# Token-major q features turned by DMA transposes for three of eight batches, and a new order from step 781 on, in a fused linear-attention and FFN kernel

## The chip, the cores and the metric

The kernel runs on one core of a Trainium2 chip. The time is that of the core, in microseconds (us) of the device. TensorE (PE) does the matmuls, VectorE (DVE) and ScalarE (ACT) the element-wise work, GpSimd (POOL) and SyncE (SP) start most of the DMA transfers here. Each engine takes its instructions in the order in which they were issued to it.

## The reference

Linear attention with an exponential feature map ("hedgehog"), 8 batches of 8 heads with 576 tokens and a head size of 64, 128 features; then an FFN with a squared relu over all 4608 tokens, 512 to 2048 to 512.

```python
def phi(x):
    proj = np.einsum('bhsd,df->bhsf', x, w_phi)
    proj = proj - np.max(np.abs(proj), axis=-1, keepdims=True)
    return np.concatenate([np.exp(proj), np.exp(-proj)], axis=-1)
q_p, k_p = (phi(q), phi(k))
kv = np.einsum('bhsf,bhsd->bhfd', k_p, v)
z = np.sum(k_p, axis=2)
num = np.einsum('bhsf,bhfd->bhsd', q_p, kv)
den = np.einsum('bhsf,bhf->bhs', q_p, z)[..., None] + 1e-06
attn = num / den                      # then x: [4608, 512], heads side by side
h = np.maximum(x @ w_in, 0.0)
return h * h @ w_out
```

For q the maximum of a token is the same in numerator and denominator but for the sign of the projection, so the kernel takes exp(+proj) and exp(-proj) without subtracting and corrects the second relative to the first by a small factor, exp(-2 max), per token and head.

## The kernel before

**Staging.** Batch b's k, q and v are loaded on POOL's queue (L253, L261, L273), in pieces, into double buffers `xk`, `xq`, `xv` (index b % 2), as tokens by head features in bf16. From batch 2 on one crossbar DMA on SP (L338) turns all of k, another all of q, into `kT` and `qT`: 18 blocks of 128x128, in which the two halves of the 128 rows hold two heads' features of 64.

**Attention of a batch** works on five blocks of tokens and heads, c = 0 to 3 (1024 columns each: 128 tokens by 8 groups) and c = 4 (half as wide, the last 64 tokens of each head).
- k: `project` (L354) makes the projection with tokens on the rows, DVE takes its maximum (L409), ACT the two exponentials `kp`, `kn` (L415), DVE scales v (L442), and PE adds up the 65-column products into kv (L472, L477).
- q: `qmax_ops` projects the q block with tokens on the rows (L354, "Pq"), DVE takes the maximum (L514, "Mq") and the PSUM banks are given back; ACT makes the correction factor `en` (L521). `q_ops` then projects the same q block a second time with features on the rows (L549, "Fq": two matmuls with up to 512 columns, on the upper and the lower 64 rows of the array), because the out heads need features on the rows; ACT takes the two exponentials from PSUM into `qp` and `qn` (L564), rings of three buffers.
- `out_ops`: eight matmuls over `qp` (L579, "NA"), DVE multiplies by `en` in PSUM (L591, "SA"), eight more over `qn` ("NB"), then the reciprocal of the denominator (L599, "rd") and the product (L603, "xo"). From batch 1 on a crossbar DMA on SP (L637) turns `xo` into `xT` (c = 0 to 3) or, for the left-over tokens, `xS` (c = 4); four blocks each.

**FFN.** Chunks of 512 tokens: chunk b takes all of batch b's `xT`, chunk 8 the 64 left-over tokens of every batch. `ffn_in` (L719, four matmuls of 512 columns per step, 16 steps) goes through relu (ACT L694 or DVE L696) and the square (DVE L703) to `h2`; `ffn_out` (L784, four matmuls per step, 16 steps) goes through a copy (L195, L197) to a store on SP (L803). Chunk 0 is taken tile by tile (L730).

**What sets the order.** The functions only record steps in a `Plan`. `ORDER` is a list of all 1731 steps written out in the code: the steps are issued in that order, and each engine keeps its part of it. `BASES` names the PSUM banks of each group, `STATES` the engine where there is a choice, and `GATES` makes a load wait for a chosen ACT or DVE step besides its buffer. Across engines only data and buffers make a step wait. So PE weaves FFN matmuls of chunk b-1 and b-2 between the attention steps of batch b and b-1. SP's queue holds, in `ORDER`'s sequence, the k and q transposes of the next batch, the `xT` and `xS` transposes of this one, and the stores.

Of the kernel before, what the change touches and what calls it, by code (L numbers as in the profile page):

```python
# [7 lines left out]
F32 = mybir.dt.float32  # L8
# [3 lines left out]
ACT = mybir.ActivationFunctionType  # L12
# [12 lines left out]
def dve_cost(n):  # L25
    return n / 960 + 0.064, n / 960 + 0.150 + SEM
# [85 lines left out]
def kernel(  # L112
# [41 lines left out]
    def sb(name, shape, dt=BF16):  # L154
        return pool.tile([P, *shape], dt, name=name)

    def ring(name, n, shape, dt=BF16):
        return [sb(f"{name}{i}", shape, dt) for i in range(n)]
# [19 lines left out]
    qp, qn = ring("qp", NQP, [8 * P]), ring("qn", NQP, [8 * P])  # L178
# [4 lines left out]
    mkn = sb("mkn", [36], F32)  # L183
# [132 lines left out]
    def attention(b):  # L316
# [181 lines left out]

        def qmax_ops(c):
# [17 lines left out]
            add("DVE", dve_cost(2 * n * Fd), fn, r=[pj], w=[("mq", s2, c)], closes=pj, what="Mq")  # L517
# [13 lines left out]

        qfeat = {}
# [128 lines left out]
        else:  # L661
# [17 lines left out]
            kv_ops(3)  # L679
            for c in range(5):  # L680
                qmax_ops(c)
            for c in range(5):
                q_ops(c)
                out_ops(c)
# [320 lines left out]
```

## Time and profile before

| | |
|---|---|
| time of the runs | 355.16 us median of 3 (354.82 to 355.61) |
| span of the profiled execution | 353.0 us, 8396 instructions |
| span of the profile against the median | 2.16 us below it; what lies around the span is not in the profile |
| L784 `ffn_out` matmuls | 128.4 us, x527 recorded |
| L719 `ffn_in` matmuls | 106.1 us, x448 recorded |
| L564 exponentials `qp`, `qn` | 37.4 us each, x40 each |
| L514 maximum of q | 44.1 us, x40 |
| L549 second projection of q | 14.9 us, x80 |
| transposes on SP: `kT`, `qT`, `xT`, `xS` | 6, 6, 28, 7 |
| medians from issue to landing of these | 5.5, 5.3, 2.7, 4.8 us |

The page gives busy times by engine over the span, and the chain of work that ended last. Rows of a line give its count, its busy time and the mean time of one. A matmul's own duration (379 ns for 512 columns) overlaps with the next one's, so what a step costs TensorE is read from the chain, where each piece has its start, its length and its count. A DMA's issue occupies the queue of the engine that starts it; its landing is counted from the start of the issue.

### The profile page before, as it was taken

Reading aid. Unit: us, or ns where it says so; the run is one execution under the profiler, and the core shown is the slowest. Engines: PE = TensorE matmul, PEld = TensorE weight load, DVE = VectorE, ACT = ScalarE, POOL = GpSimd, SP = SyncE. Lnnn points to the kernel's source line nnn. Section 1 sums busy time; section 2 is a strip of 40 time slices with the busy share of each in tenths; the row PEclk is TensorE's granted clock in tenths of the full one; section 3 lists DMA queues with packets and bytes.
Section 4 is the critical chain, followed back from the end, with each engine's and each line's share of the span. In section 5 each row is a group of like instructions: output and inputs, shape, how many; then the busy total and the mean of one; then the engine's idle time right before and its main releaser. Section 6 shows DMA issues by size and latency. Waiting matters only on the chain.

```text
span 353.0 us, 8396 instructions
## 1 busy us (share of the span) xinstructions
PE 340.7 (97%) x3367; PEld 192.2 (54%) x3400; DVE 276.1 (78%) x524; ACT 226.8 (64%) x428; POOL 96.6 (27%) x144
## 2 busy tenths in 40 slices
PE   8889999999999999999999999999999999999995
PEld 5679875544654554545445654455555544444452
DVE  4999998899979988989678888799988727736210
ACT  4999887499688875785678577869676211340301
POOL 8745350488429300297001820000000000000000
PEclk9999999999999999999999999999999999999999
DMA  9999999899989976899354995600211211010105
GB/s 102 177 200 202 196 107 155 134 142 175 182 169 150 155 141 155 160 111 158 79 129 84 120 187 111 146 20 21 53 40 53 47 51 48 30 59 2 59 3 176
DMA packets 96101, 39.59 MB, mean 112 GB/s; under 512 B 64576, under 2 KB 91584, under 8 KB 96064
## 3 DMA queue, kind: packets, MB, share of 16 engines
q0 software_dynamic: 45216, 18.36, 45.6%
q1 hardware_dynamic: 50528, 20.42, 26.5%
q8 instruction: 26, 0.43, 0.5%
q10 hardware_dynamic: 320, 0.30, 0.3%
q14 instruction: 11, 0.09, 0.1%
HBM read 36.77 MB, written 9.44 MB: 131 GB/s over the span
## 4 chain that ended last, share of the span: by engine, by line
PE 79%; DVE 8%; ACT 6%; DMA 3%; issue 2%; SPq 0%; POOL 0%; DVEq 0%; ACTq 0%; POOLq 0%
PE psum L784 30%; PE psum L719 28%; PE psum L579 5%; PE psum L354 4%; PE psum L472 3%; PE psum L730 3%; PE psum L549 2%; DVE va L442 2%; DMA xq<-in_q_dram 1%; DVE mq L514 1%; ACT kp L415 1%; ACT kn L415 1%; DMA out_dram<-ot 1%; DVE mk L388 1%; DVE h L703 1%
## 5 line engine op out<-in xcount | busy, mean ns | idle before, releaser
L784 PE MATMUL psum<-wout,h 128*128 128x512 bf16 x527 | 128.4, 379 | 3.2 <-issue 1.3
L719 PE MATMUL psum<-xT,win 128*128 128x512 bf16 x448 | 106.1, 379 | 0.1
L694 ACT ACTIVATE hr<-psum 128x512 bf16<-128x512 f32 x96 | 55.3, 596 | 46.3 <-PE psum L719 24.3
L784 PEld LDWEIGHTS <-h 128*128 128x128 bf16 x560 | 50.2, 98 | 55.2 <-issue 2.0
L719 PEld LDWEIGHTS <-win 128*128 128x128 bf16 x512 | 47.4, 97 | 53.7 <-issue 3.1
L703 DVE TENSOR_TENSOR h<-hr 128x512 bf16<-128x512 bf16 x143 | 55.9, 415 | 16.4 <-ACT hr L694 15.6
L564 ACT ACTIVATE qp<-psum 128x1024 bf16<-128x1024 f32 (+1 forms) x40 | 37.4, 940 | 21.9 <-PE psum L549 21.5
L514 DVE TENSOR_REDUCE mq<-psum 128x8 f32<-128x1024 f32 (+1 forms) x40 | 44.1, 1110 | 4.0 <-PE psum L354 3.2
L409 DVE TENSOR_REDUCE mk<-psum 128x8 f32<-128x1024 f32 (+1 forms) x35 | 38.1, 1110 | 3.1 <-PE psum L354 3.1
L415 ACT ACTIVATE kp<-psum 128x1024 bf16<-128x1024 f32 (+1 forms) x35 | 32.8, 937 | 11.6 <-DVE mk L409 8.9
L564 ACT ACTIVATE qn<-psum 128x1024 bf16<-128x1024 f32 (+1 forms) x40 | 37.4, 939 | 1.3 <-PE psum L579 1.0
L696 DVE TENSOR_SCALAR hr<-psum 128x512 bf16<-128x512 f32 x48 | 32.6, 686 | 6.5 <-PE psum L719 5.2
L253 POOL DMA_DIRECT2D xv<-in_v_dram x26 | 19.4, 763 | 51.3 <-DVE va L442 48.0
L415 ACT ACTIVATE kn<-psum 128x1024 bf16<-128x1024 f32 (+1 forms) x35 | 32.8, 936 | 0.0
L442 DVE TENSOR_TENSOR va<-xv,va 64x256 bf16<-64x256 bf16 (+2 forms) x68 | 30.4, 462 | 1.6 <-ACT va L434 0.8
L591 DVE TENSOR_TENSOR psum<-psum,en 128x520 f32<-128x520 f32 (+1 forms) x40 | 27.6, 699 | 3.9 <-PE psum L579 2.5
L603 DVE TENSOR_TENSOR xo<-psum,rden 128x512 bf16<-128x512 f32 (+1 forms) x40 | 27.3, 686 | 1.0 <-DVE rden L599 0.2
L197 ACT ACTIVATE ot<-psum 128x512 f32<-128x512 f32 x18 | 10.7, 595 | 27.1 <-PE psum L784 27.1
L195 DVE COPY ot<-psum 128x512 f32<-128x512 f32 x17 | 11.5, 684 | 15.2 <-PE psum L784 7.9
L253 POOL DMA_DIRECT2D xk<-in_k_dram x28 | 20.6, 743 | 8.4 <-ACT va L428 4.0
L472 PE MATMUL psum<-va,kp 128*128 128x65 bf16 x256 | 19.6, 193 | 0.8 <-DVE va L442 0.4
L472 PE MATMUL psum<-va,kn 128*128 128x65 bf16 x256 | 19.6, 193 | 0.0
(69 smaller groups left out, 403.4 us busy)
## 6 DMA issues: line engine op xcount, KB each, us to landing
out_dram<-ot SPq DMA_DIRECT2D x32, 256.0 KB, 2.7
xk<-in_k_dram POOLq DMA_DIRECT2D x26, 128.0 KB, 4.3
xq<-in_q_dram POOLq DMA_DIRECT2D x24, 128.0 KB, 5.5
xv<-in_v_dram POOLq DMA_DIRECT2D x24, 128.0 KB, 4.2
win<-in_moe_w_in_dram POOLq DMA_DIRECT2D x4, 512.0 KB, 11.3
wout<-in_moe_w_out_dram POOLq DMA_DIRECT2D x4, 512.0 KB, 11.7
xq<-in_q_dram POOLq DMA_DIRECT2D x4, 256.0 KB, 5.8
xv<-in_v_dram POOLq DMA_DIRECT2D x2, 512.0 KB, 9.3
```

The costliest lines, as they stand in the source:

```text
L253: pin(nc.gpsimd.dma_start(out=x[:, a * 512 : z * 512].rearrange("p (h x) -> p h x", x=4 * D), in_=src[b][2 * a : 2 * z, 0:512, :].rearrang ...
L409: pin(nc.vector.tensor_reduce(out=mk_view(g), in_=ps2(pj)[:, :, : n * Fd].rearrange("p e (i f) -> p e i f", f=Fd), axis=AX.X, op=ALU.max, ...
L415: pin(nc.scalar.activation(out=dst[slot][:, :, :n, :].rearrange("p e i f -> p e (i f)"), in_=ps2(pj)[:, :, : n * Fd], func=ACT.Exp, scale= ...
L442: pin(engine().tensor_tensor(out=t[:, :, :D].rearrange("p m (x c) -> p m x c", c=2), in0=x.rearrange("p (m x c) -> p m x c", m=n, c=2), in ...
L472: pin(nc.tensor.matmul(out=o[:, sg, hi, :], lhsT=(kp, kn)[sg][kgroup[pr]][:, j % 2, 2 * hi + j // 2, :], rhs=va[s2][sg][:, 8 * pr + 4 * hi ...
L514: pin(nc.vector.tensor_reduce(out=mqb[:, c, :, :n], in_=ps2(pj)[:, :, : n * Fd].rearrange("p e (i f) -> p e i f", f=Fd), axis=AX.X, op=ALU ...
L564: pin(nc.scalar.activation(out=o, in_=i_, func=ACT.Exp, scale=sgn))
L694: pin(nc.scalar.activation(out=hr[sl], in_=ps1(g), func=ACT.Relu))
L696: pin(nc.vector.tensor_scalar(out=hr[sl], in0=ps1(g), scalar1=0.0, scalar2=None, op0=ALU.max))
L703: pin(engine().tensor_tensor(out=dst, in0=i_, in1=i_, op=ALU.mult))
L719: pin(nc.tensor.matmul(out=o, lhsT=win[mc // 4][:, kc, mc % 4 * P : (mc % 4 + 1) * P], rhs=x, start=(kc == 0), stop=(kc == KC - 1)))
L784: pin(nc.tensor.matmul(out=ps1(g), lhsT=h2[c % 2][mc // 4][:, mc % 4, tt * P : (tt + 1) * P], rhs=wout[mc // 4][:, mc % 4, :], start=(mc = ...
```

## The change

For batches 5, 6 and 7 (`LATE = 5`):
- `qmax_ops` keeps the token-major projection in PSUM after the maximum; ACT takes the two exponentials from it, into the load buffer of the same batch that has already been turned: `xk` for even c, `xq` for odd c. Then SP turns both at once by a crossbar DMA of 16 blocks into the feature ring (for c = 4 by two of 4 blocks). `q_ops` is not called: its 15 groups of two matmuls are gone. The transpose waits for the exponentials and for the ring buffer, the next use of the load buffer (by the block c+2, and by the loads two batches later) for the transpose.
- Each block's maximum and `out_ops` are recorded one after the other instead of all maxima first; the number of steps stays the same.

For all batches `qp` and `qn` become the two halves of one ring `qf` of three buffers, and a tile `mkn` that nothing used goes. `ORDER` is a new one from its 781st step on (about 131 us in the trace before), with the `BASES` and `STATES` that belong to it. In `GATES` two entries differ: 1365 (a small load of q of batch 7) waits for 1030 instead of 1027, the same ACT step under its new number, and 1371 (a small load of v of batch 7) for 1377, the first k exponential of batch 7, instead of 1043.

```diff
+    LATE = 5
-    qp, qn = ring("qp", NQP, [8 * P]), ring("qn", NQP, [8 * P])
+    qf = ring("qf", NQP, [2, 8 * P])
+    qp, qn = [t[:, 0, :] for t in qf], [t[:, 1, :] for t in qf]
...
-    mkn = sb("mkn", [36], F32)
...
-            add("DVE", dve_cost(2 * n * Fd), fn, r=[pj], w=[("mq", s2, c)], closes=pj, what="Mq")
+            turned = b >= LATE
+            add("DVE", dve_cost(2 * n * Fd), fn, r=[pj], w=[("mq", s2, c)] + [pj] * turned, closes=None if turned else pj, what="Mq")
+            if turned:
+                slot = qslot[0] % NQP
+                qslot[0] += 1
+                qfeat[c] = slot
+                src, qx = (("xk", xk), ("xq", xq))[c % 2]
+                qe = qx[s2][:, : 16 * P].rearrange("p (u x) -> p u x", u=2)
+                held = of(src, b, (0, 1, 2, 3, "s"))
+                for u, sgn in enumerate((1.0, -1.0)):
+                    def fn(u=u, sgn=sgn):
+                        i_, o = ps2(pj)[:, :, : n * Fd], qe[:, u, : 2 * n * Fd]
...
+                        pin(nc.scalar.activation(out=o, in_=i_, func=ACT.Exp, scale=sgn))
+                    add("ACT", act_cost(2 * n * Fd), fn, r=[pj], w=[pj] + held, closes=pj if u else None, what="Eq")
+                def fn():
+                    if c == 4:
+                        for u in range(2):
+                            pin(nc.sync.dma_start_transpose(out=qf[slot][:, u, : 4 * P].rearrange("f (x p) -> f x p", p=P),
+                                                            in_=qe[:, u, : 4 * Fd]))
+                    else:
+                        pin(nc.sync.dma_start_transpose(out=qf[slot].rearrange("f u (x p) -> f (u x) p", p=P),
+                                                        in_=qx[s2][:, : 16 * P]))
+                add("SP", (2.5 if c < 4 else 2.0, 0), fn, r=held, w=[("qp", slot), ("qn", slot)],
+                    dma=(3.2 * n / 4, HW_IN, "x", "kq"), what="Xf")
...
+            if b < LATE:
+                for c in range(5):
+                    qmax_ops(c)
             for c in range(5):
-                qmax_ops(c)
-            for c in range(5):
-                q_ops(c)
+                if b < LATE:
+                    q_ops(c)
+                else:
+                    qmax_ops(c)
                 out_ops(c)
```

On SP's queue the changed order puts, from there on: batch 4's four `xT`; batch 5's features c=0, batch 6's k and q, batch 5's c=1 to 4; batch 5's `xT` (c=1, 0, 3, 2); batch 7's k; batch 6's features c=1, 0, 3, 2, between them batch 6's `xT` c=0, then c=1, batch 7's q, c=3; batch 6's features c=4 and `xT` c=2; batch 7's features c=0 to 4; batch 7's `xT` (c=2, 1, 3, 0), with the `xS` transposes and the stores between.

More of the change, by code (lines that the diff above doesn't have):

```diff
@@ L497, in q_ts @@
             return [(8 * (c // 2) + 4 * (c % 2) + i) if pe_in else 8 * (c % 2) + 2 * i + c // 2 for i in range(4)]
+        qfeat = {}
         def qmax_ops(c):
@@ L516, in fn @@
                     axis=AX.X, op=ALU.max, apply_absolute_value=True))
-            add("DVE", dve_cost(2 * n * Fd), fn, r=[pj], w=[("mq", s2, c)], closes=pj, what="Mq")
+            turned = b >= LATE
[11 more added lines that the diff above has]
+                        if c == 4:
+                            o, i_ = o.rearrange("p (i e f) -> p e i f", e=2, f=Fd), i_.rearrange("p e (i f) -> p e i f", f=Fd)
+                        else:
+                            o = o.rearrange("p (e x) -> p e x", e=2)
+                        pin(nc.scalar.activation(out=o, in_=i_, func=ACT.Exp, scale=sgn))
+                    add("ACT", act_cost(2 * n * Fd), fn, r=[pj], w=[pj] + held, closes=pj if u else None, what="Eq")
+                def fn():
+                    if c == 4:
+                        for u in range(2):
[6 more added lines that the diff above has]
+                    dma=(3.2 * n / 4, HW_IN, "x", "kq"), what="Xf")
             if c < 4:
@@ L530, in qmax_ops @@
                     add("ACT", act_cost(4), fn, r=[("mq", s2, 4)], w=[("en", s2, 4, hi)], what="en")
-        qfeat = {}
         def q_ops(c):
@@ L679, in attention @@
             kv_ops(3)
+            if b < LATE:
+                for c in range(5):
+                    qmax_ops(c)
             for c in range(5):
-                qmax_ops(c)
-            for c in range(5):
-                q_ops(c)
+                if b < LATE:
+                    q_ops(c)
+                else:
+                    qmax_ops(c)
                 out_ops(c)
@@ L948 @@
     '7762205543351613247724322302602306674447442731320126074760270660422244446264622606176160063720462403'
-    '6376440226246040224115440556605777123504024764140002202442402462567677750767766755006425602422242222'
-    '6400041712301603166777067742404660026444202224400017210165317677737366646061634664004006640006224525'
-    '2454225454357220664133466404400220620232550535444304162615557154625737570741465213753727542242756523'
-    '160'
+    '6376440226246040224115440556605777123504024764140002202442402262567677750767766755204205410045062426'
+    '0664224775446104061020510106426177640624244241032170310667601716700240233720440644667745476653763010'
+    '2631260442223066600400642345222624372543324021104562724003135227670272366751147320753641'
 )
@@ L955 @@
     '0000000000000000010100110100110100010010000010000010000000000000100000001000100010100111000000001000'
-    '0010000000001010000000100010000101010000100010010001001001111111000110010000001000110100100101000010'
-    '011000000101100101001001111100011100100101111010010100010000111111000100001'
+    '0010000000001010000000100010000101011000000001000100000011101000100001001000001110000000100111001001'
+    '010000000101001010110011000000101000010110000000100001010000110101000110000'
 )
```

166 rows, old and new, of tables (GATES, ORDER) are left out of this document.

## The prediction

> **What bounds the kernel now.** I read the busy times first, then the chain of waits that ended last, then the idle time stage by stage.
>
> ```profile
> PE 340.7 (97%) x3367; PEld 192.2 (54%) x3400; DVE 276.1 (78%) x524; ACT 226.8 (64%) x428; POOL 96.6 (27%) x144
> PEclk9999999999999999999999999999999999999999
> PE 79%; DVE 8%; ACT 6%; DMA 3%; issue 2%; SPq 0%; POOL 0%; DVEq 0%; ACTq 0%; POOLq 0%
> PE psum L784 30%; PE psum L719 28%; PE psum L579 5%; PE psum L354 4%; PE psum L472 3%; PE psum L730 3%; PE psum L549 2%; DVE va L442 2%; DMA xq<-in_q_dram 1%; DVE mq L514 1%; ACT kp L415 1%; ACT kn L415 1%; DMA out_dram<-ot 1%; DVE mk L388 1%; DVE h L703 1%
> ```
>
> TensorE is busy for 97% of the span and is 79% of the chain; the two FFN matmuls alone are 58%, and L549, the projection that the change drops for three batches, is 2%. So an instruction that leaves TensorE shortens the kernel by its whole time, unless a wait takes its place. How little waiting there is now, the windows over the part whose order changes show; their columns are the length, the busy time of PE, PEld, DVE, ACT, POOL (with counts), the granted clock, DMA share and GB/s.
>
> ```profile
> 133.00:160.00 27.00, 26.63 (x250) 13.64 (x251) 24.32 (x38) 19.47 (x36) 12.50 (x19) 1.00 0.86 141
> 160.00:190.00 30.00, 29.00 (x274) 15.14 (x275) 24.50 (x46) 21.21 (x41) 5.06 (x8) 1.00 0.76 125
> 190.00:220.00 30.00, 29.52 (x307) 15.84 (x308) 24.91 (x47) 20.55 (x36) 10.89 (x16) 1.00 0.84 120
> 220.00:250.00 30.00, 29.67 (x288) 15.75 (x289) 26.62 (x50) 23.62 (x47) 0.00 (x0) 1.00 0.28 68
> 250.00:297.00 47.00, 46.63 (x406) 24.24 (x409) 33.59 (x67) 21.89 (x39) 0.00 (x0) 1.00 0.18 47
> ```
>
> Length less PE busy is 0.37, 1.00, 0.48, 0.33 and 0.37 us: 2.55 us idle in 164 us. There is no old stall worth having; any new one adds to the time. DVE is at 90% in the first window and ACT at 65 to 79%: both have room, DVE little. From 297 on attention is over and the FFN runs alone; the change reaches that part only through its start.
>
> **What it removes.** Each L549 group is a pair of matmuls that run on the two row halves together. Its price is the step of the chain in which it stands.
>
> ```profile
> 203.78 0.22 PE psum L549 x2
> ...
> 209.04 0.86 PE psum L784 x4
> 209.91 0.25 PE psum L579 x8
> 210.15 0.33 PE psum L354 x8
> ```
>
> A pair costs 0.22 us. Batches 5 to 7 have 15 pairs, four with 512 columns and one with 256 per batch: 12 × 0.22 + 3 × 0.11 = 2.97, say **−2.9 us**. Everything else TensorE does stays. The same rows give the yardstick for what follows: a full matmul is 0.86 / 4 = 0.216 us, a group of eight out heads (L579) 0.25, of eight projections (L354) up to 0.33.
>
> **What it moves between ACT and DVE.** The 30 exponentials keep their shape and number; they now read the token-major projection that the maximum already read, so it stays in PSUM for two exponentials more, while the second pair of banks, which held the feature-major projection for the same two, is not opened at all.
>
> ```profile
> 247.98 1.02 ACT L564 ACTIVATE qp<-psum 128x1024 bf16<-128x1024 f32 x1 [1.39 <-PE psum L549]
> 248.90 1.02 ACT L564 ACTIVATE qn<-psum 128x1024 bf16<-128x1024 f32 x1
> ```
>
> Two follow each other in 0.92 us, so 1.8 us of holding moves from one bank pair to another. Cost 0. But the exponentials of block c+2 overwrite the buffer that the transpose of block c reads, so they wait for its landing, with their bank held and ACT's later relus queued behind; I allow +0.4 us (0 to 1.8, one pair of exponentials late). The merged ring of features and the unused tile that goes cost no instruction.
>
> **What it adds: 18 crossbar transposes on SP** (12 of 16 blocks; 6 of 4 blocks). The trace has 18 and 4 blocks:
>
> ```profile
> L338 SPq DMA_TRANSPOSE kT<-xk x1: 2401/2401/2401, 141.7 to 141.7; - x1
> DMA to landing us min/median/max: 4.6/4.6/4.6
> ...
> L338 SPq DMA_TRANSPOSE kT<-xk x1: 4903/4903/4903, 111.1 to 111.1; - x1
> DMA to landing us min/median/max: 11.0/11.0/11.0
> ```
>
> So 16 blocks hold SP for some 2.4 us and land after 4.6; among other traffic it can be 4.9 and 11.0. For SP that is an estimated 12 × 2.4 + 6 × 1.2 = 36 us more over three batches, on a queue that has room, but in order: a transpose that waits stops the xT transposes behind it, and with them the next FFN chunk.
>
> In sentences of its own: the Trainium skill, "DMA: Bandwidth & Descriptors", section "Latency and other measured facts", gives crossbar transposes an effective 261 GB/s, which for the 512 KB of 16 blocks would be about 2.0 us (an estimate); the clean row says 4.6 us, and the row decides. By the page's figure the ring's wait below would be 0 and the sum 0.3 us smaller.
>
> **The waits that this makes.** What an xT transpose takes depends on the loads beside it. Its rows, with POOL's burst of loads:
>
> ```profile
> L637 SPq DMA_TRANSPOSE xT<-xo x1: 1191/1191/1191, 178.3 to 178.3; - x1
> DMA to landing us min/median/max: 2.3/2.3/2.3
> ...
> L637 SPq DMA_TRANSPOSE xS<-xo x1: 1171/1171/1171, 202.7 to 202.7; - x1
> DMA to landing us min/median/max: 5.8/5.8/5.8
> ...
> L637 SPq DMA_TRANSPOSE xT<-xo x1: 1257/1257/1257, 203.9 to 203.9; - x1
> DMA to landing us min/median/max: 6.5/6.5/6.5
> ...
> L637 SPq DMA_TRANSPOSE xT<-xo x1: 2208/2208/2208, 206.8 to 206.8; - x1
> DMA to landing us min/median/max: 5.8/5.8/5.8
> ...
> L637 SPq DMA_TRANSPOSE xT<-xo x1: 1191/1191/1191, 210.0 to 210.0; - x1
> DMA to landing us min/median/max: 3.1/3.1/3.1
> ```
> ```profile
> 199.29 1.41 POOL L253 DMA_DIRECT2D xv<-in_v_dram  x2 [1.42 <-ACT hr L694]
> ...
> 203.40 0.71 POOL L253 DMA_DIRECT2D xk<-in_k_dram  x1
> 204.09 0.72 POOL L273 DMA_DIRECT2D xq<-in_q_dram  x1
> ```
>
> Alone 2.3 us; within a burst of loads 5.8 and 6.5, and 2 us after its last issue (204.1 + 0.7) still 5.8; 5 us after, 3.1. Before it, an out-head block goes through DVE:
>
> ```profile
> L603 DVE TENSOR_TENSOR xo<-psum,rden 128x512 bf16<-128x512 f32 (+1 forms) x40 | 27.3, 686 | 1.0 <-DVE rden L599 0.2
> L599 DVE RECIPROCAL rden<-psum 128x8 f32<-128x8 f32 (+1 forms) x40 | 7.9, 199 | 6.9 <-PE psum L579 6.6
> ```
>
> *Chunk 4.* In the changed order, between batch 4's last needed out heads (c=1) and chunk 4's first matmul TensorE has 16 full matmuls and three small attention groups: 16 × 0.216 + 0.6 = 4.1 us. The path beside it: reciprocal 0.20, xo 0.69, one xT issue ahead 1.2, landing 2.3 = 4.4 us. Alone it is 0.3 us late, with 5.8 us 3.8 late. The remaining loads of batch 6 stand on POOL up to there; I take the lower middle, **+1.5** (0.3 to 3.8).
>
> *Chunk 5.* After batch 5's c=2 out heads come 24 full matmuls and three projections, 24 × 0.216 + 3 × 0.33 = 6.2 us. The path: 0.20, two xo's 1.38, one issue, of which 0.5 lies beside the second xo, 0.7, landing 2.3 = 4.6: clean it is hidden. But the k and q buffers of batch 7 are the ones that batch 5 now writes its exponentials into, so batch 7's k and q loads cannot start before batch 5's last feature transposes land, and twelve loads then follow each other just as these xT transposes go. With 5.8 to 6.5 us the path is 8.1 to 8.8, and the wait 1.9 to 2.6. I take the row of the burst, **+2.0** (0 to 2.6).
>
> *Ring of three feature buffers.* The transpose for c=3 cannot start before c=0's second out heads are done. In batch 5, 4.9 us of TensorE work (20 full matmuls, a projection, a head group) stand between; the path is 4.6. I take +0.3 (0 to 6.1, the 11.0 row).
>
> *Chunk 6.* The two transposes of batch 6's c=4 stand on SP directly ahead of its last xT: 2.4 us more in front. Cover 4.8 us, path 0.9 + 2.4 + 2.3 = 5.6 if SP reaches them late, 3.2 if early. I take +0.5 (0 to 0.8).
>
> *Old waits.* Of the 1.81 us that TensorE idles from 160 to 250 some are of the old order and go; half, **−0.9** (−1.8 to 0).
>
> Sum: −2.9 + 0.4 + 1.5 + 2.0 + 0.3 + 0.5 − 0.9 = **+0.9 us**; I add 0.4 for ACT and DVE, which get the exponentials in shorter stretches (0 to 1): +1.3. The profiled execution spans 353.0 us, so 354.3; the runs' median is 355.16, 2.16 above the span for what lies around it, and I carry the difference over: **356.5 us**.
>
> **The rivals.**
>
> *The transfers hide.* Xo and loads do not meet, each crossbar lands in 2.3 or 4.6 us: the chunk waits are 0.3 and 0, and of the other terms only 0.4 + 0.3 remain. −2.9 + 0.3 + 0.7 = −1.9: 353.3; with the old waits gone too 352.3, and the TensorE saving alone gives 352.3 as well. For it: the clean landings at 141.7 and 178.3, and an idle DMA (share 0.18 to 0.28) from 220 on. Against it: nothing in the changed order but buffer reuse keeps batch 7's loads away from batch 5's xT, and it puts them together.
>
> *Pile-up at batch 7's k.* Its loads wait for batch 5's last transposes (two issues, 3.9 us in all), then 12 issues of 0.72 (8.6), a landing under load of 5.8, the k transpose 4.6: 22.9 us, while TensorE has 24 groups of four full matmuls (20.8) and 2 us of small ones before the first k projection of batch 7: 22.8. From there on every microsecond decides: with the 11.0 us row, 6.4 more, and batch 6's feature transposes queue behind it on SP. 356.5 + 5 = 361.5, as part of the wait lies beside chunk 5's.
>
> *No change.* The chunk waits just eat the saving, or batch 5 to 7 are bound by DVE (26.62 of 30 us busy from 220 to 250), which loses nothing: 355.2.
>
> *A clock that falls.* The granted clock is 9 in all slices and 1.00 in every window above, with up to 1.00 us idle in one. A wait of 3.8 us before chunk 4 would be longer than any here. If TensorE ran at half its rate after it for as long as it waited, 3.8 us of work would take 7.6: 356.5 + 2.3 + 3.8 = 362.6. No trace here shows the clock fall, so this has little chance.
>
> In sentences of its own: the Trainium skill, "TensorE: Matmul & The Clock Gate", section "Part 1: The HAM clock gate (the "warmup" mystery)", says that the clock follows the activity seen in windows of about 3.4 us and is halved when it is low; that is the rule by which this rival would come about, and no row shows it.
>
> **How the numbers follow.** About 0.2% (0.7 us) is what a measurement of this kernel can tell from no change. Chances: the forecast 0.42 (its own range 355.9 to 359.4: the top has chunk 4's wait at 3.8 and chunk 5's at 2.6, which is 2.9 more); transfers hidden 0.36; no change 0.10; pile-up 0.10; clock 0.02. Faster is the second alone, 0.36; same 0.10; slower 0.42 + 0.10 + 0.02 = 0.54. The time is that of the forecast, 356.5. The range starts at 352.4, where nearly all of the hidden case is in, and ends at 360.3, which leaves out the pile-up at full price.
>
> **What would show it.** L549 loses 30 matmuls, and exponentials that read a projection of q directly appear beside those of L564. If I am right, TensorE idles before the first L719 of chunks 4 and 5, released by a crossbar DMA on xT with landings of 4 to 6 us, POOL issuing batch 7's k and q loads at the same time. If those landings are 2.3 us and TensorE's idle time in 133 to 297 stays near 2.5 us, the second case holds. A k transpose of batch 7 that lands late, with DVE's k maximum waiting, is the third. Wrong altogether would be a time above 361 with TensorE waiting on ACT, or one below 352.

## The result and the profile after

| | before | after |
|---|---|---|
| median of 12 runs | 355.46 us (354.82 to 357.31) | 357.23 us (355.58 to 359.60) |
| span of the profiled execution | 353.0 us | 355.4 us |

The ratio is 1.0052, 95% interval [1.0033, 1.0072]: the change makes the kernel slower by half a per cent, 1.8 us. The forecast was 356.5, 1.3 us slower.

The page of the changed kernel: busy times, the granted clock in 40 slices, SP's DMA queue, and the chain by engine.

```profile
PE 339.2 (95%) x3333; PEld 191.8 (54%) x3370; DVE 266.7 (75%) x509; ACT 233.1 (66%) x443; POOL 96.7 (27%) x144
PEclk9999999999999999999999899999999999999999
q1 hardware_dynamic: 78752, 27.50, 40.9%
PE 76%; DVE 9%; DMA 5%; ACT 5%; issue 3%; POOL 0%; DVEq 0%; ACTq 0%; POOLq 0%
```

TensorE's share of the chain fell from 79 to 76%, DMA's rose from 3 to 5%, and one slice has a lower clock. The same windows as before the change, columns as there:

```profile
133.00:160.00 27.00, 25.59 (x254) 13.32 (x256) 22.59 (x38) 22.49 (x42) 9.97 (x15) 1.00 0.88 144
160.00:190.00 30.00, 28.90 (x320) 16.02 (x320) 26.66 (x48) 24.88 (x49) 5.51 (x9) 1.00 1.17 158
190.00:220.00 30.00, 27.59 (x213) 13.53 (x214) 21.97 (x41) 18.28 (x31) 8.14 (x12) 0.94 1.10 152
220.00:250.00 30.00, 29.55 (x283) 15.85 (x287) 23.16 (x44) 20.76 (x42) 4.86 (x7) 1.00 0.71 132
250.00:297.00 47.00, 46.68 (x412) 24.65 (x417) 34.02 (x67) 22.66 (x43) 0.00 (x0) 1.00 0.58 115
```

Length less PE busy is now 1.41, 1.10, 2.41, 0.45 and 0.32, together 5.69 us against 2.55: 3.1 us more idle time, almost all in two windows, 133 to 160 and 190 to 220. The clock of 0.94 over 30 us is another 0.06 × 30 = 1.8 us. Less the 2.9 us of matmuls that went, that is +2.0; the spans differ by 2.4. Part of the 2.4 lies behind TensorE: the last copy of the output ends at 351.0 us instead of 349.4, 1.6 us later, and the other 0.9 us is in the last stores and the end of the program. The new order holds the steps of the end too, at which the forecast did not look. What TensorE waited for from 133 to 297 us, in the waits view (total, times, longest):

```profile
PE psum L607 <- DMA qf<-xq: 2.1, 1, 2.1
PE psum L751 <- DMA xT<-xo: 0.9, 1, 0.9
PE psum L607 <- DVE psum L619: 0.5, 1, 0.5
PE psum L473 <- DVE mq L517: 0.5, 1, 0.5
```

The longest is new: out heads (L607) that wait for a feature transpose. SP's and ACT's timelines and the chain show how it came about (start, length, operation):

```profile
185.16 2.53 SPq L544 DMA_TRANSPOSE qf<-xk  x1
193.57 2.81 SPq L544 DMA_TRANSPOSE qf<-xq  x1
```
```profile
189.88 1.02 ACT L536 ACTIVATE xq<-psum 128x1024 bf16<-128x1024 f32 x1
190.93 1.08 ACT L536 ACTIVATE xk<-psum 128x512 bf16<-128x512 f32 x2
191.90 1.03 ACT L536 ACTIVATE xq<-psum 128x1024 bf16<-128x1024 f32 x1
```
```profile
192.13 0.88 PE psum L751 x4
...
193.57 6.99 DMA qf<-xq
200.61 0.42 PE psum L607 x8
```

Batch 5's transpose for c=3 is issued at 193.57, when both c=0's second out heads (193.4) have given the ring buffer back and its own exponentials (192.93) are there; it lands after 6.99 us. Behind the wait the clock falls (windows of 2 us; the column ahead of the last two is the granted clock):

```profile
198.00:200.00 2.00, 0.49 (x3) 0.00 (x0) 0.00 (x0) 0.01 (x1) 0.00 (x0) 1.00 0.83 38
200.00:202.00 2.00, 1.39 (x21) 0.92 (x22) 0.86 (x2) 0.00 (x0) 0.88 (x2) 0.99 0.62 125
202.00:204.00 2.00, 2.00 (x15) 0.90 (x12) 1.48 (x3) 0.02 (x1) 2.00 (x4) 0.50 1.04 137
204.00:206.00 2.00, 2.00 (x19) 1.02 (x17) 1.43 (x4) 0.97 (x3) 2.00 (x4) 0.66 1.07 102
206.00:208.00 2.00, 1.95 (x10) 0.87 (x9) 1.57 (x4) 0.41 (x1) 1.85 (x3) 1.00 1.92 164
```

From 202 to 206 us TensorE is fully busy at 0.50 and 0.66: 2 × 0.50 + 2 × 0.34 = 1.7 us lost. Batch 7's loads start when the transpose has landed, as the forecast has it, and lie beside batch 5's xT (POOL's timeline, then the chain):

```profile
201.12 0.71 POOL L274 DMA_DIRECT2D xq<-in_q_dram  x1 [8.31 <-DMA qf<-xq]
...
212.14 2.75 PE psum L751 x12
```

In this trace chunk 5's first matmul comes at 212.1, and its last xT lands at 208.1 + 3.9 = 212.0. No wait is left there, because the matmuls between c=3's out heads and chunk 5 ran slowly: the 1.7 us of the clock stand where the wait for xT would have been, as e1 shows below.

### The profile page after: what moved, and what is told of

The parts are those of the page before. It is cut to its first block, busy times and chain, and to the rows that moved or that the text cites. A ratio compares the mean times of both kernels' runs of the same rounds, so it can differ in the third digit from the quotient of the medians.

```text
span 355.4 us, 8395 instructions
## 1 busy us (share of the span) xinstructions
PE 339.2 (95%) x3333; PEld 191.8 (54%) x3370; DVE 266.7 (75%) x509; ACT 233.1 (66%) x443; POOL 96.7 (27%) x144
## 4 chain that ended last, share of the span: by engine, by line
PE 76%; DVE 9%; DMA 5%; ACT 5%; issue 3%; POOL 0%; DVEq 0%; ACTq 0%; POOLq 0%
PE psum L816 29%; PE psum L751 27%; PE psum L607 5%; PE psum L355 4%; PE psum L473 3%; PE psum L762 3%; DVE mq L517 2%; DVE va L443 2%; DMA qf<-xq 2%; DMA xq<-in_q_dram 1%; PE psum L577 1%; ACT qf L592 1%; DMA xT<-xo 1%; ACT kp L416 1%; DVE mk L389 1%
## 5 line engine op out<-in xcount | busy, mean ns | idle before, releaser
L751 PE MATMUL psum<-xT,win 128*128 128x512 bf16 x448 | 109.4, 383 | 1.1 <-DMA xT<-xo 0.9
L726 ACT ACTIVATE hr<-psum 128x512 bf16<-128x512 f32 x98 | 57.0, 597 | 47.9 <-PE psum L751 41.8
L816 PEld LDWEIGHTS <-h 128*128 128x128 bf16 x560 | 51.2, 98 | 55.1 <-issue 0.5
L592 ACT ACTIVATE qf<-psum 128x1024 bf16<-128x1024 f32 (+1 forms) x50 | 45.9, 946 | 8.4 <-PE psum L577 8.1
L728 DVE TENSOR_SCALAR hr<-psum 128x512 bf16<-128x512 f32 x46 | 31.3, 687 | 18.6 <-PE psum L751 16.4
L607 PEld LDWEIGHTS <-qf 128*128 128x128 bf16 x640 | 28.7, 98 | 17.1 <-issue 2.8
L607 PE MATMUL psum<-kv,qf 128*128 128x65 bf16 x640 | 31.5, 194 | 2.8 <-DMA qf<-xq 2.1
L198 ACT ACTIVATE ot<-psum 128x512 f32<-128x512 f32 x28 | 16.6, 596 | 24.9 <-PE psum L816 23.5
L274 POOL DMA_DIRECT2D xq<-in_q_dram x24 | 17.2, 720 | 31.1 <-ACT va L429 15.7
## 6 DMA issues: line engine op xcount, KB each, us to landing
wout<-in_moe_w_out_dram POOLq DMA_DIRECT2D x4, 512.0 KB, 11.9
```

The source lines that it names most:

```text
L592: pin(nc.scalar.activation(out=o, in_=i_, func=ACT.Exp, scale=sgn))
L607: pin(nc.tensor.matmul(out=o[:, u // 4, u % 4 * D1 : (u % 4 + 1) * D1], lhsT=(qp, qn)[sg][slot][:, u * m : u * m + P], rhs=kv_sb[s2][:, h ...
L726: pin(nc.scalar.activation(out=hr[sl], in_=ps1(g), func=ACT.Relu))
L728: pin(nc.vector.tensor_scalar(out=hr[sl], in0=ps1(g), scalar1=0.0, scalar2=None, op0=ALU.max))
L751: pin(nc.tensor.matmul(out=o, lhsT=win[mc // 4][:, kc, mc % 4 * P : (mc % 4 + 1) * P], rhs=x, start=(kc == 0), stop=(kc == KC - 1)))
L816: pin(nc.tensor.matmul(out=ps1(g), lhsT=h2[c % 2][mc // 4][:, mc % 4, tt * P : (tt + 1) * P], rhs=wout[mc // 4][:, mc % 4, :], start=(mc = ...
```

## The experiments

All times are medians; ratios are to the kernel before, on the same chip; runs of different chips are compared by their ratios. In the order of steps `move(a, b)` puts step a directly ahead of step b. "Lag" in the expectations is the start of a step in the trace less the TensorE work that stands ahead of it in the order (by the prices of the prediction), so that a rise of the lag is time lost.

### What held the c=3 features

**e1: a fourth feature buffer.**

```diff
-    NQP = 3
+    NQP = 4
-    otl = sb("otl", [DM], F32)
+    otl = xk[0][:, : 2 * DM].bitcast(F32)
```

> The changed kernel with four feature buffers in the ring instead of three (the small output tile of the end shares a load buffer to make room). My theory: batch 5's transpose for c=3 was held by two things that end 0.6 us apart, the ring buffer (c=0's second out heads, 193.4 us) and its own exponentials (192.9 us), so a larger ring alone brings it forward by 0.6 us at most: TensorE still waits 1.3 to 2.1 us for it before c=3's out heads, time 356.4 to 357.2. Rival, the ring is what holds it: the wait and the slow clock behind it go, 2.1 + 1.7 us, time about 353.5.

355.84 us, 1.0036 [1.0012, 1.0059]. The transpose went out at 192.4 instead of 193.6 (TensorE is 0.6 us ahead there), landed after 7.3 us, and TensorE still waited:

```profile
PE psum L751 <- DMA xT<-xo: 3.1, 3, 1.6
PE psum L607 <- DMA qf<-xq: 1.9, 1, 1.9
```

So the ring alone did not hold it. The median is lower by more than expected, though the intervals of the two kernels overlap. And the wait for xT before chunk 5 is there: this run's clock stayed at 1.00, TensorE came earlier to chunk 5 and waited 1.6 us.

```profile
199.81 0.43 PE L607 MATMUL psum<-kv,qf 128*128 128x65 bf16 x8 [1.94 <-DMA qf<-xq]
...
211.20 2.75 PE L751 MATMUL psum<-xT,win 128*128 128x512 bf16 x12 [1.56 <-DMA xT<-xo]
```

From c=3's out heads to chunk 5's first matmul it is 11.4 us here, with the clock up and a wait, and 11.5 us in the changed kernel, with the clock down and no wait (200.6 to 212.1). So the wait for the features and the one for xT add up, and in the changed kernel's trace the slow clock only took the place of the second.

**e2: work in the idle time.** 20 small matmuls on a constant tile ahead of the c=3 out heads (step 1067).

```diff
+FILL.update({1067: (4, 20, 0)})
```

> The changed kernel with 20 matmuls of 248 columns on a constant tile ahead of batch 5's c=3 out heads, in a bank that is free there; they do nothing for the output. By 248 / 2.4 that is an estimated 20 x 0.103 = 2.1 us, the time that TensorE idled there. Theory: the granted clock of 0.50 to 0.66 from 202 to 206 us in the changed kernel follows from that idle time, so it stays at 1.00, and the time falls by up to 1.7 us (355.5) although the wait itself is still there. Rival: the clock falls for another reason, it is as low as before, and the time is the same or longer (357.2 and more).

358.77 us, 1.0112 [1.0086, 1.0139]: slower, a miss. From 200 to 210 us the clock stayed at 1.00, as the theory has it, but then:

```profile
200.00:210.00 10.00, 9.95 (x97) 5.42 (x96) 8.46 (x17) 4.26 (x9) 6.72 (x10) 1.00 1.34 156
210.00:220.00 10.00, 7.39 (x40) 3.06 (x40) 4.67 (x10) 6.46 (x10) 0.00 (x0) 0.83 1.20 205
```
```profile
PE psum L751 <- DMA xT<-xo: 4.2, 3, 2.6
```

Chunk 5 now waits 2.6 us for its xT, which lands after 6.0 us, and the clock falls behind that wait instead. That fits a clock that follows the idle time, but one trace does not show it: seven of the changed kernel's 12 runs have no such fall either. The wait that the forecast put at chunk 5 is there once the clock stays up on the way to it. The four runs with a mean clock above 0.9965 average 358.4, also above the changed kernel's; beside chunk 5's, this trace has a wait of 0.9 us for chunk 6's xT.

**e3: the c=3 out heads later.**

```diff
+move(1067, 1134)
+move(1068, 1134)
+move(1056, 1068)
```

In this order the second out heads of batch 5's c=3 come ahead of the first, which start the sum anew: their part is left out of that block.

> The changed kernel with batch 5's c=3 out heads three steps later on TensorE, behind two FFN steps and c=2's out heads that were ready (1.97 us of work). Theory: the wait of 2.1 us is covered and the clock stays up, 2.1 + 1.7 us less: 353.5 to 354.5. Rival: the later out heads delay batch 5's xT by as much, and chunk 5 waits instead: 356 to 357.2.

357.47 us, 1.0055 [1.0038, 1.0073]. The rival was right: the wait for the features is gone, and chunk 5 waits for xT, with a clock of 0.83 from 210 to 220 us.

```profile
PE psum L751 <- DMA xT<-xo: 3.0, 2, 2.6
```
```profile
L665 SPq DMA_TRANSPOSE xT<-xo x2: 1190/1200/1210, 203.9 to 205.2; - x2
DMA to landing us min/median/max: 5.8/5.8/5.9
```

The two last xT land after 5.8 and 5.9 us, the value taken from the burst before the change.

### What TensorE's share was worth

**e5: the 15 pairs put back.**

```diff
                 o = ps2(g)
+                if what == "Pq" and b >= LATE:
+                    for u in range(2):
+                        r = slice(64 * u, 64 * u + 64)
+                        pin(nc.tensor.matmul(out=o[:, u, : n * P].rearrange("f (i x) -> f i x", x=P), lhsT=wphi2[r, :],
+                                             rhs=xt[r, ts[0] : ts[-1] + 1 : ts[1] - ts[0], :], start=True, stop=True))
```

> The changed kernel with the 15 pairs of feature-major matmuls put back ahead of the token-major projections of q (batches 5 to 7); what they write is overwritten at once. If TensorE sets the time, this costs what the removal was to save: 12 x 0.22 + 3 x 0.11 = 2.9 us, 360.1 us against 357.2. Rival: where TensorE waits for landings anyway part of it is hidden; four of the pairs stand in stretches before the c=3 and chunk 5 waits, so 0.9 us less, 359.2.

360.84 us, 1.0133 [1.0099, 1.0166]. By the ratios, 1.0133 against 1.0052, that is 2.9 us more than the changed kernel, by the medians 3.6; the runs with a clock above 0.9965 alone average 359.9 (four) against 356.6 (seven), 3.2 us. This fits the full price. The four lie between 358.7 and 361.1, though, so that the rival's 2.0 us is not excluded.

### What slows xT

**e6: out heads later, chunk 5 covered.** As e3 with both out heads moved, and two ffn_out steps (1312, 1316) with the squares they need ahead of chunk 5's first step (1283).

```diff
+move(1067, 1134)
+move(1068, 1134)
+move(1056, 1068)
+move(1069, 1057)
+move(1312, 1283)
+move(1146, 1202)
+move(1142, 1202)
+move(1150, 1202)
+move(1153, 1304)
+move(1154, 1187)
+move(1316, 1283)
```

> The changed kernel with batch 5's c=3 out heads (both of them, with their product) behind two FFN steps and c=2's, and two ffn_out steps of chunk 4 (1.73 us) moved ahead of chunk 5's first matmul, the relu and squares they need ahead of batch 6's maxima. Theory: the 2.1 us wait for the c=3 features is covered; chunk 5 then waits for its last xT, which lands in 5.8 us under batch 7's loads, 2.9 us in the run with the heads later, less the 1.73 = 1.2 us; a clock of 1.00 throughout: lag at the end about 29.5 instead of 32.2, span 352.7, time 354.5. Rival: DVE's moved squares make the k maxima of batch 6 late and batch 6's attention waits instead: 356 to 357.

354.83 us, 0.9985 [0.9971, 1.0000]; span 353.5, clock 1.00 throughout. The wait at chunk 5 is 1.9 us, not 1.2, because c=2's xT landed after 6.9 us this time. By the ratios the run is 2.4 us below the changed kernel: covering the one wait and part of the other, with a mean clock of 0.996 or more in all 12 runs, gives back more than the 1.8 us that the change had cost.

**e7: e6 without the loads beside xT.**

```diff
+move(1366, 1358)
...
+move(1363, 1358)
+GATES[1366] = 1149
```

> As the one before, and batch 7's first seven loads wait for chunk 4's 15th relu (about 210 us), so that none is under way while batch 5's xT go over. Theory: xT of c=3 and c=2 land in 2.3 to 2.8 us instead of 5.8, and chunk 5 starts without a wait (its path alone is 4.6 us against 6.2 + 1.7 of cover); batch 7's k is turned 4 to 6 us later and its first projection waits 0 to 4 us. Rival: the landing times come from the transposes queued on each other, then they stay at 4 us or more without the loads.

359.46 us, 1.0109 [1.0090, 1.0129]. The same two transposes, in e6 and then in e7 (issue times, then landings):

```profile
L665 SPq DMA_TRANSPOSE xT<-xo x2: 1197/1224/1252, 204.1 to 205.4; - x2
DMA to landing us min/median/max: 5.7/6.3/6.9
```
```profile
L665 SPq DMA_TRANSPOSE xT<-xo x2: 1191/1200/1210, 204.3 to 205.6; - x2
DMA to landing us min/median/max: 2.3/2.3/2.4
```

Issued at the same times, they land in 2.3 and 2.4 us instead of 5.7 and 6.9: the loads make the difference, not the other transposes. Chunk 5 starts without a wait for xT. The price is at batch 7's k, for which the waits view has:

```profile
PE psum L355 <- DMA kT<-xk: 3.1, 1, 3.1
```

Those 3.1 us, and a clock that falls behind them (0.50 from 226 to 228 us), are more than the wait saved.

**e8: also chunk 4's loads earlier, and the ring of four.** e1 and e6, and of batch 6's loads the two of v that waited for batch 4's scaling go last, and a small one of q loses its gate.

```diff
+move(1172, 1366)
+move(1171, 1366)
+GATES.pop(1169)
```

> As e6, with four feature buffers, and batch 6's q and k loads ahead of two v loads that wait for batch 4's scaling, so that they go out from 155 instead of 158.8 us and end before chunk 4's last xT goes over at 166.9. Theory: that xT lands in 2.4 to 3.1 instead of 3.9 us, chunk 4's wait of 0.9 to 1.3 us shrinks by 0.9, the larger ring gives 0.6: 353.0, below the kernel before (355.2). Rival: the transposes of chunk 4 are slowed by each other, and the loads do not matter: as e6.

354.29 us, 0.9973 [0.9957, 0.9989]: faster than the kernel before, though not by the 2 us expected. Chunk 4's last xT, in the changed kernel and in e8:

```profile
L665 SPq DMA_TRANSPOSE xT<-xo x1: 1210/1210/1210, 166.9 to 166.9; - x1
DMA to landing us min/median/max: 3.9/3.9/3.9
```
```profile
L665 SPq DMA_TRANSPOSE xT<-xo x2: 1190/1200/1210, 166.2 to 167.5; - x2
DMA to landing us min/median/max: 2.3/2.3/2.3
```
```profile
PE psum L751 <- DMA xT<-xo: 2.0, 2, 1.6
```

Chunk 4's wait is gone; the two for xT that e8 still has are chunk 3's, 0.4 us, and chunk 5's, 1.6. **e12**, the same kernel beside e11:

> The kernel of e8 once more, beside e11 on one chip: 354.3 again, ratio to the kernel before 0.996 to 0.999; the rival is that e8 was a good chip, ratio 1.0 or above.

353.96 us, 0.9967 [0.9955, 0.9979].

**e9: batch 7's k loads first, the others behind a gate.**

```diff
+move(1359, 1364)
...
+move(1363, 1372)
+GATES[1366] = 1149
```

> As e8, and of batch 7's loads the six of k go out first; the four others (q, and one of v of batch 6) and all behind them wait for chunk 4's 15th relu (about 210 us). Theory: only six issues instead of thirteen lie beside batch 5's last two xT, so that these land in 3 to 4.5 instead of 5.8 and 6.6 us, and chunk 5's wait (1.6 to 2.0 us) shrinks to 0 to 0.5, while batch 7's k is turned at 212 to 215 as before: 352.5 to 353.0. Rival: six loads slow the transposes as much as thirteen; the wait stays, 354.3, or batch 6's late v takes its place.

357.54 us, 1.0075 [1.0058, 1.0093]. The xT landed in 2.3 us, and chunk 5's wait went, as expected. But the gated loads (207.5 to 212.2 us) then met batch 7's k transpose:

```profile
L339 SPq DMA_TRANSPOSE kT<-xk x1: 6546/6546/6546, 209.0 to 209.0; - x1
DMA to landing us min/median/max: 14.4/14.4/14.4
```
```profile
211.44 11.91 DMA xv<-in_v_dram
```

It took 14.4 us, and a load of v 11.9 us, for which DVE's scaling waited. The collision had only been moved.

### The lag before chunk 4

When TensorE has done 127 us of its work (at about 150 us), the new order has lost 1.6 us more than the old one. The chain of the changed kernel just before:

```profile
140.90 3.48 DMA out_dram<-ot
...
144.47 0.70 DVE ot L196
```

**e4: two stores ahead of batch 5's k transpose**, those of chunk 1 (the expectation calls it chunk 2; `move(727, 979)`, `move(745, 979)`).

> The changed kernel with two stores of chunk 2 put on SP ahead of batch 5's k transpose and batch 3's xT, so about 8 us earlier. Theory: in the changed kernel they went out at 140.9 us, behind four transposes, landed at 144.4, and DVE's copy into their output buffer waited for that with batch 4's k and q maxima behind it, 1.1 us of TensorE idle from 140 to 150 and 2.3 us of lag by 152; with them first that is gone, 355 to 356. Rival: the lag comes from DVE's own load or from the loads, and moves only to the next wait: 357 and more.

356.45 us, 1.0050 [1.0028, 1.0071]: no gain that these intervals show. The store is out of the chain, and chunk 3 starts no earlier, for now it waits for xT that stand behind the k transpose and the stores:

```profile
140.99 3.21 DMA xT<-xo
```

**e10: e8 with batch 3's xT ahead of batch 5's k transpose** (`move(979, 745)`; the k projection of batch 5 and its maximum and first exponential, 981 to 983, ahead of 901).

> As e8, and on SP batch 5's k transpose goes behind batch 3's three xT again, as before the change; batch 5's first k projection goes behind two FFN steps of chunk 3. Theory: of the 2.0 us that the kernels with the new order lose by 146 us against the kernel before, most is chunk 3 waiting for xT that stand behind the k transpose (3.6 us on SP); they land at 139 to 140 instead of 143.6, chunk 3 starts 1 to 1.5 us earlier, time 353.0 to 353.5. Rival: DVE's maxima set that stretch, which come no earlier: 354.3 or more, with the wait at batch 5's k projection.

355.77 us, 1.0016 [0.9999, 1.0032], slower than e8. xT land by 139.1, and DVE waits for the store again (140.90, 4.14 us), then TensorE for the bank of the moved projection.

**e11: both** (`move(727, 673)`, `move(745, 673)`, `move(979, 906)`; 981 to 984 behind batch 4's maximum of c=0).

> As e8, and on SP two stores of chunk 2, then batch 3's three xT, then batch 5's k transpose; batch 5's first k projection with its maximum and exponentials stands behind batch 4's maximum of c=0. The two runs that moved only the stores (e4) or only the xT (e10) showed chunk 3's start held by the other of the two, at 144.2 and 145.1 us. Theory: with both moved chunk 3 starts at 141 to 142 us and the lag of about 24 us that the new order has by 146 us is 22 to 22.5, as before the change: 352.5 to 353.5. Rival: a third wait of the same length stands there (ACT with the exponentials of batch 4's k, or the bank of the moved projection): 354.3 or more.

354.98 us, 1.0006 [0.9982, 1.0029], no better than e8, and slower than e8's kernel beside it on the same chip (e12, 0.9967). Lags in us at five places, worked out from the traces:

```
TensorE work so far      127    148    176    184    end
before                  21.9   22.3   24.7   24.8   27.9
after                   23.5   25.3   29.9   30.1   32.2
e6                      23.7   25.2   26.0   28.6   30.5
e8                      24.1   24.7   26.2   28.5   30.5
e11                     22.6   25.1   26.1   27.1   29.9
```

At 127 us of work e11 has won 1.5 us on e8, and at 148 it has lost them again:

```profile
PE psum L355 <- DVE mq L517: 1.3, 1, 1.3
```

The rival was right there: a third wait, for the maximum that frees the projection's bank.

## Why the prediction was right

The direction and the mechanism (transposes that land among loads cost more than the matmuls saved) hold. That the size comes out so close (1.3 us forecast, 1.8 measured) is in part luck: one wait is seven times as long as forecast, a loss on SP and one at the end were missing, and against these stand terms that did not show. By its steps:

- **What it removes, −2.9 us:** right. Putting the pairs back costs 2.9 to 3.6 us (e5).
- **Chunk 4, +1.5 us:** 0.9 us of wait in the trace, with a landing of 3.9 us, between the two rows taken for it. e8 shows that the loads caused it.
- **Chunk 5, +2.0 us:** right in place, cause and size, 1.6 to 2.6 us in e1 to e5 (e6 and e8 still have 1.9 and 1.6, with 1.73 us more of cover). It is not seen in the changed kernel's own trace, where the slow clock stood in its place. The wait for the features does not hide it: e1 and e4 have both, 1.9 + 1.6 and 1.7 + 2.0 us.
- **Ring of three buffers, +0.3 us (0 to 6.1):** the term that was mis-sized. It is 2.1 us, and 1.9 and 1.7 in e1 and e4. The step "the path is 4.6" took the clean landing; it was 7.0, with the two c=4 transposes issued directly behind it and two loads shortly ahead. And the ring is only one of two things that end together (e1). Which neighbour makes the landing 7.0 was not tried by itself; e1 and e8, which issued it a microsecond earlier, had 7.3 and 7.6.
- **Chunk 6, +0.5, and ACT, +0.4 and +0.4:** no wait of TensorE over 0.2 us is put down to ACT in the view of the changed kernel, and the two of 0.5 us for DVE lie before 160 us, ahead of the first exponentials of the new kind (169.0). Chunk 6's wait shows in e2 alone, 0.9 us. (ACT's share in the prediction's windows is 47 to 79%, not 65 to 79; no term rests on it.)
- **Old waits, −0.9:** the before's wait for DVE's output copy, 0.7 us, is gone after; the rest stays open.
- **Missing:** batch 5's k transpose on SP ahead of batch 3's xT and the stores, the 1.6 us of lag at 127, of which e11, with the stores and the xT ahead again, has 0.9 back. The forecast priced what the new transposes hold up on SP, but not what a moved old one does. Missing too is the end of the kernel, 0.9 us of the span: "the change reaches that part only through its start" does not hold.
- **A clock that falls, 0.02:** too low, and its condition wrong. It was to need a wait of 3.8 us; 2.1 us was enough. Of the 12 runs of the changed kernel five have a mean clock of 0.993 to 0.995 and average 358.3, the other seven 356.6, so a low clock goes with 1.6 us more, and is part of the spread of 4 us. In the profiled run, the fastest of the five (357.21), the fall cost next to nothing, as it took chunk 5's wait away; where it fell in the other four no trace shows. The Trainium skill, "TensorE: Matmul & The Clock Gate", section "Part 1: The HAM clock gate (the "warmup" mystery)", halves the clock after at least one idle window of about 3.4 us; the 0.50 agrees, the length of the idle time does not.

The hidden case (352.3 to 353.3) fails because the transposes do meet loads, in every kernel here that did not move them apart. No pile-up at batch 7's k came about in the changed kernel (its transpose landed after 5.3 us), but e9 shows that its 11.0 us row was no upper bound.

## What to carry to other kernels

Work moved from a matmul to a DMA transpose is free only if its landing is covered at the price it has among the loads of that moment; here that is 5.8 to 6.9 us instead of 2.3 for the last xT, and the loads were released by the landing of the feature transposes, just as xT went out. When several waits end within a microsecond of each other, removing one shows the next (e1 to e4, e10, e11): move all of them or put independent matmuls ahead of the waiting one, which is what made e8 faster than both kernels. A short idle stretch of TensorE can cost 1.7 us more through the clock, unless a wait behind it would have taken the same time.

## What the runs showed of the hardware

- The granted clock fell, by 1.7 us of TensorE's work each time (2 us at 0.50 and 2 at 0.66 in the changed kernel), after waits of 1.7 (e10), 2.1 (the changed kernel), 2.2 (e5), 2.6 (e2, e3) and 3.1 us (e7), and did not after 1.7 (e9), 1.9 (e1, e6), 2.0 (e4) and 2.3 us (e12): no single length decides.
- A crossbar transpose and loads slow each other: 4 blocks 2.3 us (e7) to 8.4 (e12), 18 blocks 4.6 us (before) to 14.4 (e9), a load of v 11.9 us (e9) against a median of 4.6 in the changed kernel.
